# Top-k attention and a gated feed-forward on one core: crossbar transposes queued two slots later, raw weights loaded three chunks ahead, more feed-forward pieces a step

## The chip, the cores and the metric

The kernel runs on one core of a Trainium2 chip. Five engines work side by side, each through its own instructions in order: TensorE (PE) multiplies, VectorE (DVE), ScalarE (ACT) and GpSimd (POOL) work element by element, and SyncE (SP) issues the transfers. They meet through semaphores. The metric is the time of one execution in microseconds (us), as the median of several runs.

## The reference, cut to what matters

```python
# attention: q, k, v are (8, 8, 576, 64) float32
scores = scale * q @ k.T                                  # (8, 8, 576, 576)
kth    = partition(scores, -32)[..., -32]                 # the 32nd largest of each row
scores = where(scores >= kth, scores, -1e9)
attn   = exp(scores - max(scores)); attn /= sum(attn) + 1e-9
x      = (attn @ v) as (4608 tokens, 512)
# feed-forward: w_in (512, 2048) and w_out (2048, 512) are float64
h   = x @ w_in
g   = h * clip(h + 3, 0, 6) / 6
out = g @ w_out                                           # (4608, 512) float32
```

## The kernel before

**Units.** A `Duo` is 128 query rows (a *full* duo) or the 64 leftover rows (a *rest* duo) of four heads, held as two *units* u = 0, 1 of two heads each. There are 80 duos: ten for each of eight batches, of which eight are full and two (the third and the eighth) are rest. The main loop takes *step* m for duo m, and works on its neighbours in the same step: it makes the scores of duo m+1 (`scores`, PE into one large PSUM tile that ACT copies out), finds the 32 largest of each row of duo m (`top`, DVE), and carries duo m-1 and m-2 through softmax and the product with v.

**Slots.** A step has eight slots, `top(0)` to `top(7)`, four for each unit. In a slot DVE takes the eight largest values of each row (`max`, L245) and, in three slots of four, replaces them (`match_replace`, L249); a full duo has two row tiles per unit, a rest duo one. All other work of the step is written between the slots, and this order is the order on every engine, since the kernel schedules by hand.

**From scores to x.** `exp(u)`: POOL makes the threshold and shift (L260 to L262), ACT applies both and sums (L265, L270), POOL adds the epsilon to the sum `den` (L275). `weights(u)`: DVE takes the reciprocal of `den` (L284), POOL scales the rows (L287) and splits their words into two 16-bit halves in tile `e16` (L296), and SP transposes `e16` into `t16` with a crossbar transpose (L299). `join(u)`: ACT puts the halves together in `eT` (L305). `values(m-2)`: PE multiplies by v (L325), and ACT copies the result to `xT` or `xr` (L332).

**Feed-forward.** When 128 or 256 tokens of x are complete they are queued as a block of 16 or 32 *pieces*. A piece is about the same amount of PE work each time: either a half tile of h (L349) or two steps of the output sum (L370). After each full tile of h ACT applies the ReLU (L357) and DVE, more than two pieces later, the gate (L361). `left` counts the pieces queued and not done. Each step runs `count[0]` to `count[3]` pieces at four places; `count` is picked by `level`, from `left` at the step's start. What is left when the 80 duos are done runs at the end.

**Raw weights.** The float64 weights come as 32 chunks of 512 KB. `convert` loads a chunk (`st`, L100, on SP), takes two pieces of it with ACT (L105, L108), clamps with POOL (L106), shifts and merges with two DVE instructions (L114, L115) and adds with POOL (L119). `convert_step` is called in every slot while chunks are left: it finishes an older chunk and starts the next, its load included.

**Order on SP.** SP holds the loads of k and q (`load`, L147, L151), of v (`load_values`, L159, L163), of raw chunks (L100), the crossbar transposes (L299) and the stores of the output (L382), in program order; an instruction that waits holds all that stand behind it. Tiles `st`, `landed`, `kq`, `e16`, `t16` and `eT` share one pool of 14 buffers (`kqpool`).

Of the kernel before, what the change touches and what calls it, by code (L numbers as in the profile page):

```python
# [13 lines left out]
U16 = mybir.dt.uint16  # L14
# [14 lines left out]
def kernel(  # L29
# [9 lines left out]
    nc = tc.nc  # L39
    P = nc.NUM_PARTITIONS  # L40
    B, H, S, D = q.shape
    DM, FF = moe_w_in.shape
    J = S // P
# [8 lines left out]
    def pool(name, bufs, **kw):  # L52
        return ctx.enter_context(tc.tile_pool(name=name, bufs=bufs, **kw))

    consts = pool("consts", 1)
    kqpool = pool("kq", 14)
# [37 lines left out]
    def convert(dst, src):  # L94

        st = kqpool.tile([P, 2 * WC], U32, tag="kq", name="st")
        nc.sync.dma_start(st[:], src)  # L100
        words = st[:].rearrange("p (n two) -> p n two", two=2)
        lo, hi = words[:, :, 0], words[:, :, 1]
        a = gpool.tile([P, WC], F32, tag="g", name="a")
        y = gpool.tile([P, WC], F32, tag="g", name="y")
        nc.scalar.activation(a[:], hi.bitcast(F32), AF.Abs)  # L105
        nc.gpsimd.tensor_scalar(a[:], a[:], HI_MOST, HI_LEAST, ALU.min, ALU.max)  # L106

        nc.scalar.activation(y[:], lo, AF.Copy, bias=2.0, scale=2.0**-51)  # L108
        yield

        au, yu = a[:].bitcast(U32), y[:].bitcast(U32)
        nc.vector.tensor_scalar(au, au, 3, None, ALU.logical_shift_left)  # L114
        nc.vector.scalar_tensor_tensor(  # L115
            out=yu, in0=hi, scalar=0x80000000, in1=yu,
            op0=ALU.bitwise_and, op1=ALU.bitwise_or,
        )
        nc.gpsimd.tensor_tensor(  # L119
            dst.bitcast(I32), a[:].bitcast(I32), y[:].bitcast(I32), ALU.add  # L120
        )

    def weight_chunks():
        win, wout = moe_w_in.bitcast(U32), moe_w_out.bitcast(U32)
        for f in range(0, FF, WC):
            for g in range(NHP):
                rows = slice(g * P, (g + 1) * P)
                yield w_in[:, g, f : f + WC], win[rows, 2 * f : 2 * (f + WC)]
        for c in range(NFC):
            rows = slice(c * P, (c + 1) * P)  # L130
            yield w_out[:, c, :], wout[rows, :]
# [3 lines left out]
    class Pair:  # L135


        def __init__(self, b, hp):
            self.b, self.hp = b, hp
            self.vm, self.vr, self.kr = vms[hp], vrs[hp], krs[b % 2 * NHP + hp]  # L140
# [40 lines left out]
    class Duo:  # L181
# [6 lines left out]
        def __init__(self, pairs, qt):  # L188
            self.pairs, self.qt = pairs, qt
            self.rest = qt == J  # L190
            self.nt = 1 if self.rest else 2
            self.nb = J + 2 if self.rest else 2 * J + 1
            self.t16, self.eT = [None] * 2, [None] * 2

        def scores(self, us=(0, 1)):

# [41 lines left out]
        def top(self, u, r):  # L238

            if r == 0:  # L240
                self.m = mpool.tile([P, 2, TOP_K], F32, tag="m", name="m")
                self.wk = wkpool.tile([P, 2, S], F32, tag="wk", name="wk")
                self.cur = [self.row(u, t) for t in range(self.nt)]
            for t in range(self.nt):
                nc.vector.max(self.m[:, t, 8 * r : 8 * r + 8], self.cur[t])  # L245
            if r < TOP_K // 8 - 1:
                for t in range(self.nt):
                    wk = self.wk[:, t, :]
                    nc.vector.match_replace(  # L249
                        wk, self.m[:, t, 8 * r : 8 * r + 8], self.cur[t], LOWEST  # L250
                    )
                    self.cur[t] = wk
# [24 lines left out]
        def weights(self, u):  # L277

            d = self.den[:, u, 0 : self.nt]
            nc.vector.reciprocal(d, d)  # L284
            for t in range(self.nt):
                row = self.row(u, t)
                nc.gpsimd.tensor_scalar(  # L287
                    row, row, self.den[:, u, t : t + 1], 1.0, ALU.mult, ALU.mult
                )
            n = self.nb * P  # L290
            e16 = kqpool.tile([P, 2 * (2 * J + 1) * P], U16, tag="kq", name="e16")
            halves = e16[:, 0 : 2 * n].rearrange("p (h x) -> p h x", h=2)
            parts = [(0, S + R, 0), (S - P, S, S + R)] if self.rest else [(0, n, 0)]
            for c0, c1, to in parts:
                words = self.sc[:, u, c0:c1].bitcast(U16).rearrange("p (x h) -> p h x", h=2)
                nc.gpsimd.tensor_copy(halves[:, :, to : to + c1 - c0], words)  # L296
            t16 = kqpool.tile([P, 2 * (2 * J + 1), P], U16, tag="kq", name="t16")
            self.t16[u] = t16
            nc.sync.dma_start_transpose(t16[:, 0 : 2 * self.nb, :], e16[:, 0 : 2 * n])  # L299

        def join(self, u):

# [97 lines left out]
    left = 0  # L400
    gates = []

    def piece(count=1):
        nonlocal left
        for _ in range(count):
            while todo:
                try:
                    gates.append(next(todo[0]))
                    left -= 1
                    break  # L410
                except StopIteration:
                    todo.pop(0)
            else:
                gates.append(None)
            if len(gates) > 2:
                gate = gates.pop(0)
                if gate:
                    gate()
# [38 lines left out]
            queue(state["xT"], c0 + P, rows)  # L457

    chunks = list(weight_chunks())
    converting = []  # L460

    def convert_step(depth=1):

        while len(converting) > depth:
            next(converting.pop(0), None)
        if converting and not chunks:
            next(converting.pop(0), None)
        if chunks:
            c = convert(*chunks.pop(0))
            next(c)  # L470
            converting.append(c)

    def pair_at(m, first):

        b, at = divmod(m, per_batch)
        return pairs[b + 1][at - first] if b + 1 < B and 0 <= at - first < NHP else None

    first = pairs[0]
    first[0].load()
    convert_step(2)  # L480
    first[0].transpose()
    duos[0].scores((0,))
    first[1].load()
    convert_step(2)
    first[1].transpose()
    duos[0].scores((1,))
    first[2].load()
    convert_step(2)
    first[3].load()

    for m in range(ND + 2):
        u = duos[m] if m < ND else None
        prev = duos[m - 1] if 0 < m <= ND else None


        level = (left >= 10) + (left >= 20)
        if u and u.rest:
            count = [(1, 0, 1, 0), (1, 0, 1, 1), (1, 1, 1, 1)][level]
        else:
            count = [(2, 1, 2, 1), (2, 2, 2, 1), (2, 2, 2, 2)][level]  # L500
        depth = 2 if m < 2 else 1

        def top(r):
            if u:
                u.top(r // 4, r % 4)
            convert_step(depth)

        if prev:
            prev.exp(1)
        elif m == 0:  # L510
            first[2].transpose()
            first[3].transpose()
        if m + 1 < ND:
            duos[m + 1].scores()
        top(0)
        piece(count[0])
        p = pair_at(m, 4)
        if p:
            p.load()
        if m == 0:  # L520
            first[0].load_values()
            first[1].load_values()
        top(1)
        if prev:
            prev.weights(1)
        if m > 1:
            values(m - 2)
        if u and u.pairs[0].b and 1 <= m % per_batch <= 2:
            for p in duos[m - 1].pairs:
                p.load_values()  # L530
        piece(count[1])
        top(2)
        if prev:
            prev.join(0)
        top(3)
        if u:
            u.exp(0)
        if m == 0:
            first[2].load_values()
            first[3].load_values()  # L540
        piece(count[2])
        top(4)
        p = pair_at(m, 5)
        if p:
            p.transpose()
        top(5)
        if u:
            u.weights(0)
        piece(count[3])
        top(6)  # L550
        if prev:
            prev.join(1)
        top(7)
        if m == 3:
            piece(3)
    while todo:
        piece()
    piece(2)
# [33 lines left out]
```

## Time and profile before

| | us |
|---|---|
| median of three runs (1792.1 to 1793.2) | 1792.3 |
| the profiled execution's own time | 1793.51 |
| its span in the profile | 1791.7 |
| DVE busy (87% of the span) | 1560.9 |
| PE busy (84%) | 1502.2 |
| ACT busy (66%) | 1190.7 |
| POOL busy (41%) | 735.2 |

The profiled execution is 1.8 us longer than its span and 1.2 us above the median. Busy times are means over stages with different limits, so they are read stage by stage.

### The profile page before, as it was taken

The page shows a single profiled execution, that of the slowest core. Times are in us where ns is not written, and L with a number is a line of the kernel's source. Part 1 is how long each engine was busy: PE and PEld are TensorE (multiplying, and loading weights), DVE is VectorE, ACT ScalarE, POOL GpSimd, SP SyncE. Part 2 cuts the span into 40 slices and gives each one's busy share as a digit, 9 for nine tenths or more (in the row PEclk, how much of TensorE's full clock was granted, in tenths as well). Part 3 has the DMA queues.
Part 4 walks back from the last instruction along what each step waited for, and adds up shares of the span by engine and source line. Part 5 has one row for each costly group of instructions (what it writes and reads, how often), then busy time and mean ns, then how long its engine had stood idle before and what let it go on. Part 6 is the DMA issues. An engine that isn't in the chain of part 4 may idle for free.

```text
span 1791.7 us, 24696 instructions
## 1 busy us (share of the span) xinstructions
PE 1502.2 (84%) x8480; PEld 986.7 (55%) x8480; DVE 1560.9 (87%) x3249; ACT 1190.7 (66%) x1639; POOL 735.2 (41%) x1218
## 2 busy tenths in 40 slices
PE   5122767697999999899999899899999899998999
PEld 2012454464665656464756656565666565555575
DVE  3856899999999989999999989999999999999310
ACT  4354687777877777678777777777766877766410
POOL 2565444434444444444344444434443434444100
PEclk9555888799999999999999999999999999999999
DMA  6323343444344433535244442444244533323200
GB/s 184 90 92 121 90 100 63 80 85 92 71 82 88 92 83 54 102 78 109 49 79 90 80 88 49 108 86 91 54 101 82 92 64 73 83 54 70 46 13 12
DMA packets 450302, 144.23 MB, mean 80 GB/s; under 512 B 433280, under 2 KB 441472, under 8 KB 450176
## 3 DMA queue, kind: packets, MB, share of 16 engines
q1 hardware_dynamic: 450176, 142.65, 37.9%
q8 instruction: 67, 1.10, 0.3%
q14 instruction: 59, 0.48, 0.1%
HBM read 45.09 MB, written 9.44 MB: 30 GB/s over the span
## 4 chain that ended last, share of the span: by engine, by line
DVE 64%; PE 14%; ACT 12%; POOL 3%; issue 3%; DMA 3%; SPq 0%; ACTq 0%; POOLq 0%
DVE m L245 32%; DVE wk L249 26%; PE acc L370 7%; DVE g L361 4%; PE h L349 4%; ACT eT L305 3%; ACT sc L270 3%; ACT sc L228 2%; PE big L222 2%; ACT sc L265 2%; PE pv L325 1%; DMA st<-in_moe_w_out_dram 1%; DMA t<-e 1%; DMA st<-in_moe_w_in_dram 1%; POOL a L106 1%
## 5 line engine op out<-in xcount | busy, mean ns | idle before, releaser
L245 DVE MAX8 m<-wk 128x8 f32<-128x576 f32 x864 | 612.5, 744 | 2.0
L370 PE MATMUL acc<-w_out,g 128*128 128x512 f32 x1152 | 523.4, 602 | 6.2 <-DVE g L361 6.2
L349 PE MATMUL h<-xT,w_in 128*128 128x256 f32 (+1 forms) x2304 | 474.8, 364 | 33.6 <-DVE g L361 22.2
L349 PEld LDWEIGHTS h<-xT,w_in 128*128 128x128 f32 x2304 | 402.6, 195 | 90.9 <-issue 19.1
L305 ACT COPY eT<-t 128x2304 uint16<-128x2304 uint16 (+1 forms) x160 | 418.4, 2615 | 39.6 <-DMA t<-e 39.3
L249 DVE MATCH_REPLACE8 wk<-m,wk 128x576 f32<-128x576 f32 x576 | 423.1, 740 | 0.0
L265 ACT ACTIVATE sc<-sc,kth 128x576 f32<-128x576 f32 x288 | 209.1, 768 | 252.3 <-POOL kth L260 252.2
L370 PEld LDWEIGHTS acc<-w_out,g 128*128 128x128 f32 x1152 | 213.2, 192 | 240.0 <-issue 229.3
L296 POOL COPY e<-sc 128x2304 uint16<-128x2304 uint16 (+1 forms) x192 | 321.2, 1683 | 10.1
L287 POOL TENSOR_SCALAR sc<-sc,den 128x576 f32<-128x576 f32 x288 | 214.7, 754 | 269.4 <-DVE den L284 263.9
L325 PE MATMUL pv<-eT,vm 128*64 128x128 f32 (+1 forms) x2560 | 182.2, 285 | 127.2 <-ACT eT L305 87.6
L325 PEld LDWEIGHTS pv<-eT,vm 128*64 128x64 f32 x2560 | 148.1, 148 | 178.0 <-ACT eT L305 93.0
L270 ACT ACTIVATE sc<-sc,shift 128x576 f32<-128x576 f32 x288 | 219.2, 762 | 3.0
L275 POOL TENSOR_SCALAR den<-den 128x2 f32<-128x2 f32 (+1 forms) x160 | 35.5, 222 | 446.8 <-ACT sc L270 446.8
L245 DVE MAX8 m<-sc 128x8 f32<-128x576 f32 x288 | 203.3, 742 | 15.6 <-ACT sc L231 15.6
L249 DVE MATCH_REPLACE8 wk<-m,sc 128x576 f32<-128x576 f32 x288 | 211.5, 740 | 0.0
L222 PE MATMUL big<-kq 64*128 64x512 f32 x512 | 144.0, 685 | 73.9 <-ACT kr L179 34.6
L361 DVE SCALAR_TENSOR_TENSOR g<-g,h 128x512 f32<-128x512 f32 x144 | 96.7, 672 | 106.4 <-ACT g L357 106.2
L357 ACT ACTIVATE g<-h,three 128x512 f32<-128x512 f32 x144 | 97.1, 681 | 88.0 <-PE h L349 87.8
L222 PEld LDWEIGHTS big<-kq 64*128 64x128 f32 x512 | 48.6, 206 | 142.0 <-issue 46.4
L228 ACT COPY sc<-big 128x2048 f32<-128x2048 f32 (+1 forms) x65 | 118.4, 1822 | 11.2 <-PE big L225 10.9
L260 POOL TENSOR_SCALAR kth<-m 128x2 f32<-128x2 f32 (+1 forms) x160 | 36.5, 228 | 116.9 <-DVE m L245 116.4
(45 smaller groups left out, 996.6 us busy)
## 6 DMA issues: line engine op xcount, KB each, us to landing
landed<-in_k_dram SPq DMA_DIRECT2D x64, 128.0 KB, 2.8
landed<-in_q_dram SPq DMA_DIRECT2D x64, 128.0 KB, 2.9
st<-in_moe_w_in_dram SPq DMA_DIRECT2D x16, 512.0 KB, 5.2
vm<-in_v_dram SPq DMA_DIRECT2D x64, 128.0 KB, 2.3
st<-in_moe_w_out_dram SPq DMA_DIRECT2D x16, 512.0 KB, 5.2
out_dram<-o SPq DMA_DIRECT2D x32, 256.0 KB, 2.4
t<-e SPq DMA_TRANSPOSE x160, 4.6
landed<-in_k_dram SPq DMA_DIRECT2D x32, 32.0 KB, 2.6
```

The source lines that it names most:

```text
L222: nc.tensor.matmul(banks[:, 2 * i + hh, :], pr.qT[d, qs], pr.kT[d, :])
L245: nc.vector.max(self.m[:, t, 8 * r : 8 * r + 8], self.cur[t])
L249: nc.vector.match_replace(wk, self.m[:, t, 8 * r : 8 * r + 8], self.cur[t], LOWEST)
L265: nc.scalar.activation(row, row, AF.Prelu, bias=kth[:, t : t + 1], scale=1.0, alpha=STEEP)
L270: nc.scalar.activation(row, row, AF.Exp, bias=shift[:, t : t + 1], scale=scale, accum_out=self.den[:, u, t : t + 1],)
L287: nc.gpsimd.tensor_scalar(row, row, self.den[:, u, t : t + 1], 1.0, ALU.mult, ALU.mult)
L296: nc.gpsimd.tensor_copy(halves[:, :, to : to + c1 - c0], words)
L305: nc.scalar.copy(eT[:, 0 : self.nb, :] .rearrange("p c q -> p (c q)") .bitcast(U16) .rearrange("p (x h) -> p h x", h=2), self.t16[u][:, 0 ...
L325: nc.tensor.matmul(pv[hh * D : (hh + 1) * D, u * w : (u + 1) * w], pr.vm[:, hh, c, :] if c < J else pr.vr[:, hh, :], rhs, start=(c == 0), ...
L349: nc.tensor.matmul(h[:, (f - f0) * nt : (f - f0 + 1) * nt], w_in[:, i, f * P : (f + 1) * P], xT[:, i, 0:nt], start=(i == 0), stop=(i == NH ...
L361: nc.vector.scalar_tensor_tensor(out=g[:], in0=g[:], scalar=6.0, in1=h[:], op0=ALU.min, op1=ALU.mult)
L370: nc.tensor.matmul(acc[:], gs[f // nf][:, c0 : c0 + P], w_out[:, f, :], start=(f == 0), stop=(f == NFC - 1),)
```

## The change

Three things change. The crossbar transpose of a unit leaves `weights` and becomes `flip`: `flip(1)` of the duo before stands after `top(3)` (its `weights(1)` stands after `top(1)`), and `flip(0)` of this duo after `top(7)` (its `weights(0)` stands after `top(5)`). `t16` is allocated there too. The load of a raw chunk is split off from the start of its conversion: `land` issues loads, five of which stand ahead of the main loop, and `convert_step` starts a chunk that was loaded three calls earlier and finishes one that was started two calls earlier. The loads of the first pairs and the first conversions are ordered anew. The table of pieces per step gets a fourth level and other bounds, and three extra pieces at the end of step 3 are dropped.

```diff
@@ convert
         st = kqpool.tile([P, 2 * WC], U32, tag="kq", name="st")
         nc.sync.dma_start(st[:], src)
+        yield
@@ Duo.weights
-            t16 = kqpool.tile([P, 2 * (2 * J + 1), P], U16, tag="kq", name="t16")
-            self.t16[u] = t16
-            nc.sync.dma_start_transpose(t16[:, 0 : 2 * self.nb, :], e16[:, 0 : 2 * n])
+            self.e16[u] = e16
+
+        def flip(self, u):
+            t16 = self.t16[u] = kqpool.tile([P, 2 * (2 * J + 1), P], U16, tag="kq", name="t16")
+            n = 2 * self.nb
+            nc.sync.dma_start_transpose(t16[:, 0:n, :], self.e16[u][:, 0 : n * P])
@@ loading and converting
-    converting = []
-
-    def convert_step(depth=1):
-
-        while len(converting) > depth:
-            next(converting.pop(0), None)
-        if converting and not chunks:
-            next(converting.pop(0), None)
-        if chunks:
+    landing, converting = [], []
+
+    def land(count=1):
+
+        for _ in range(min(count, len(chunks))):
             c = convert(*chunks.pop(0))
             next(c)
+            landing.append(c)
+
+    def convert_step(depth=2):
+
+        if len(converting) >= depth or not landing:
+            for c in converting[:1]:
+                next(c, None)
+            del converting[:1]
+        if landing:
+            c = landing.pop(0)
+            next(c)
             converting.append(c)
+        land()
@@ ahead of the loop
     first[0].load()
-    convert_step(2)
+    first[1].load()
+    land(2)
     first[0].transpose()
     duos[0].scores((0,))
-    first[1].load()
-    convert_step(2)
+    convert_step()
+    first[2].load()
     first[1].transpose()
     duos[0].scores((1,))
-    first[2].load()
-    convert_step(2)
+    convert_step()
     first[3].load()
+    land()
@@ the loop
-        level = (left >= 10) + (left >= 20)
+        level = (left >= 10) + (left >= 18) + (left >= 26)
         if u and u.rest:
-            count = [(1, 0, 1, 0), (1, 0, 1, 1), (1, 1, 1, 1)][level]
+            count = [(1, 0, 1, 0), (1, 1, 1, 1), (1, 1, 1, 1), (2, 1, 2, 1)][level]
         else:
-            count = [(2, 1, 2, 1), (2, 2, 2, 1), (2, 2, 2, 2)][level]
-        depth = 2 if m < 2 else 1
+            count = [(2, 1, 2, 1), (2, 2, 2, 1), (2, 2, 2, 2), (3, 2, 3, 2)][level]
...
         top(3)
+        if prev:
+            prev.flip(1)
         if u:
             u.exp(0)
...
         top(7)
-        if m == 3:
-            piece(3)
+        if u:
+            u.flip(0)
```

## Rows read from the trace of the kernel before

**Rows 1.** The page: busy time of each engine

```profile
PE 1502.2 (84%) x8480; PEld 986.7 (55%) x8480; DVE 1560.9 (87%) x3249; ACT 1190.7 (66%) x1639; POOL 735.2 (41%) x1218
```

**Rows 2.** Windows: length; PE, PEld, DVE, ACT, POOL busy (instructions); PE clock, DMA, GB/s

```profile
59.00:107.50 48.50, 7.34 (x32) 4.11 (x32) 35.16 (x60) 18.97 (x31) 26.34 (x32) 0.50 0.39 112
107.50:154.90 47.40, 9.20 (x52) 5.71 (x52) 25.65 (x42) 21.30 (x30) 26.87 (x31) 0.54 0.38 113
154.90:199.80 44.90, 19.97 (x134) 18.70 (x136) 33.02 (x60) 22.84 (x32) 24.68 (x33) 0.65 0.31 100
...
448.00:1672.00 1224.00, 1134.23 (x6414) 746.53 (x6411) 1180.71 (x2498) 899.15 (x1226) 521.42 (x894) 0.97 0.40 80
1672.00:1792.00 120.00, 115.45 (x590) 75.94 (x588) 9.79 (x15) 18.64 (x24) 3.79 (x4) 0.99 0.06 17
```

**Rows 3.** DVE's waits from 42 to 200 us: total, times, longest

```profile
DVE a L114 <- POOL a L106: 33.1, 9, 9.7
DVE den L284 <- POOL den L275: 13.3, 5, 5.2
```

**Rows 4.** Timeline of SP's queue, 30 to 84 us: start, duration, instruction

```profile
32.61 1.01 SPq L100 DMA_DIRECT2D st<-in_moe_w_in_dram  x2
58.57 2.87 SPq L299 DMA_TRANSPOSE t<-e  x1
61.54 1.95 SPq L100 DMA_DIRECT2D st<-in_moe_w_in_dram  x4
```

**Rows 5.** Timelines of POOL, DVE and ACT, 54 to 75 us

```profile
56.33 2.21 POOL L296 COPY e<-sc 128x2304 uint16<-128x2304 uint16 x1
56.50 2.58 DVE L115 SCALAR_TENSOR_TENSOR y<-st,y 128x512 uint32<-128x512 uint32 x1
...
66.82 0.66 ACT L105 ACTIVATE a<-st 128x512 f32<-128x512 f32 x1 [13.86 <-DMA st<-in_moe_w_in_dram]
...
68.22 1.49 DVE L114 TENSOR_SCALAR a<-a 128x512 uint32<-128x512 uint32 x1 [2.65 <-POOL a L106]
...
74.12 0.17 DVE L284 RECIPROCAL den<-den 128x2 f32<-128x2 f32 x1 [3.40 <-POOL den L275]
```

**Rows 6.** The chain of work that ended last, 50 to 200 us, one piece

```profile
61.54 5.20 DMA st<-in_moe_w_in_dram
```

**Rows 7.** Timelines of ACT and DVE, the start

```profile
9.79 0.66 ACT L105 ACTIVATE a<-st 128x512 f32<-128x512 f32 x1 [7.79 <-DMA st<-in_moe_w_in_dram]
...
39.81 1.49 DVE L114 TENSOR_SCALAR a<-a 128x512 uint32<-128x512 uint32 x1 [10.84 <-POOL a L106]
```

**Rows 8.** The chain of work that ended last, at the end

```profile
1683.96 2.33 PE pv L325 x40
...
1703.66 14.29 PE h L349 x128
1717.95 13.73 PE acc L370 x32
```

**Rows 9.** DVE's waits from 200 to 1672 us

```profile
DVE den L284 <- POOL den L275: 25.7, 30, 3.9
DVE g L361 <- ACT g L357: 13.0, 11, 2.6
```

**Rows 10.** Timelines of ACT and DVE in step 28, the full step after a rest step

```profile
662.45 0.37 ACT L332 COPY xT<-pv 128x256 f32<-128x256 f32 x1 [3.30 <-PE pv L325]
...
666.07 0.60 ACT L380 ACTIVATE o<-acc 128x512 f32<-128x512 f32 x1 [3.25 <-PE acc L370]
...
671.62 0.17 DVE L284 RECIPROCAL den<-den 128x2 f32<-128x2 f32 x1 [3.91 <-POOL den L275]
```

**Rows 11.** Groups by line: busy us, mean ns of one, idle before

```profile
L115 DVE SCALAR_TENSOR_TENSOR y<-st,y 128x512 uint32<-128x512 uint32 x32 | 32.4, 1014 | 0.0
L114 DVE TENSOR_SCALAR a<-a 128x512 uint32<-128x512 uint32 x32 | 26.6, 832 | 44.3 <-POOL a L106 43.9
```

**Rows 12.** Waits of SP's queue over the span

```profile
SPq L382 <- ACT o L380: 133.7, 13, 27.6
```

More of the change, by code (lines that the diff above doesn't have):

```diff
@@ L192, in __init__ @@
             self.nb = J + 2 if self.rest else 2 * J + 1
-            self.t16, self.eT = [None] * 2, [None] * 2
+            self.e16, self.t16, self.eT = [None] * 2, [None] * 2, [None] * 2
         def scores(self, us=(0, 1)):
@@ L505, in top @@
                 u.top(r // 4, r % 4)
-            convert_step(depth)
+            convert_step()
         if prev:
```

## Prediction

> **What bounds the kernel now.** I read the page first: no engine fills the span, DVE with 1560.9 us and PE with 1502.2 us are nearest [rows 1]. A mean of 87% can hide stages with different limits, so next the windows by stage [rows 2]. Three stages show. From 59 to 199.8 us (steps 1 to 3, in which raw weights are converted beside the attention) DVE is busy 35.2 + 25.7 + 33.0 = 93.8 of 140.8 us, and PE hardly at all. From 448 to 1672 us DVE is busy 1180.7 of 1224 us and PE 1134.2: DVE sets the pace, with PE 90 us short of full. From 1672 us to the end DVE has nothing left (9.8 us of work) and PE works off the backlog, 115.5 of 120 us. So time lies in two places: DVE's 47 idle us of the first steps, and the 120 us of PE work behind the last `top`.
>
> **Why DVE idles at the start.** The waits from 42 to 200 us are 46.4 us: 33.1 for POOL's clamp of a raw chunk (L106) and 13.3 for `den` [rows 3]. Followed back, one case reads so. SP issued two raw loads at 32.61 us and then nothing until 58.57, where the transpose of step 0's `weights(0)` started: the next instruction in line was that transpose, and it waited for POOL's split, which began at 56.33 and took 2.21 us. Four raw loads came only behind it, at 61.54 [rows 4, 5]. The first of them was 5.20 us under way, on the chain that ended last [rows 6]; ACT, in order, idled 13.86 us for it, to 66.82; DVE's shift of that chunk waited 2.65 us, and the exponentials that ACT had behind the chunk came late, so that DVE waited 3.40 us more for `den` [rows 5]. This happens once for each unit of steps 0 to 3 until the loads end.
>
> **Part 1, transposes later and loads ahead, at the start: -40 us.** Nothing is removed: 32 loads, 32 conversions and 160 transposes remain. What moves is SP's order: two slots' loads now pass each transpose, and each load is issued three slots ahead of its use. A slot of step 1 without its waits is 35.2 / 8 = 4.4 us [rows 2], so a load has 13 us where it needs 5.2 [rows 6]. The transpose in turn is asked for some two slots (8.8 us) after `weights` was written, and its `join` stands three slots later, so it stays covered at the start. If all waits went, each of steps 1 to 3 would take as long as its busiest engine: 35.2 (DVE), 26.9 (POOL, next to be late in the rest step) and 33.0, together 95.1 for 140.8: -45.7, the lower end. The upper end is 0, if something else holds SP. I take the clamp waits as gone whole (33.1), since the load is what is late in each, and the `den` waits as half gone (6.6 of 13.3), because an exponential still has to pass ACT: -40.
>
> The very start is booked at nothing. ACT no longer waits to 9.79 us for the first raw chunk before it copies the first transposed pair, which can bring 3 us; but conversions now end two calls after they start instead of three, so DVE meets its wait of 10.84 us [rows 7] one slot sooner. Both ends are within 4 us.
>
> **Part 2, the tail: -26 us, and 3 back.** `left` can be followed through the loop on paper, since it depends on the code alone. Take steps 62 to 71: before, 4, 8, 8, 8, 8, 4, 8, 8, 8, 7 pieces, from a backlog of 50 to one of 43; after, 6, 10, 8, 7, 7, 6, 10, 8, 7, 6, from 41 to 30. Behind step 79, the last with a `top`, 52 pieces wait before and 37 after; 16 more come from the last values in both. That is 68 against 53 at the end: 15 fewer. In the tail a block of 128 tokens, 16 pieces, takes 14.29 + 13.73 us [rows 8], 1.75 us a piece. 15 x 1.75 = 26.3 us. (Check: 68 x 1.75 and two products with v of 2.33 are 124 us for a tail of 120.) PE enters the tail later if its last steps are fuller, by less than two pieces: 3 us back.
>
> **Part 3, the fuller steps: +15 us.** The new level is reached in 14 rest steps (6 pieces for 4) and 7 full steps (10 for 8): 42 added pieces, most of them given back as fewer pieces in the steps between. If PE has room, they are free: 0, since DVE sets the pace and PE has 90 us idle [rows 2]. If PE has none, each costs its 1.75 us: 42 x 1.75 = 73.5. What lies between shows in step 28, the full step behind a rest step. There PE was behind DVE; ACT, in order, waited 3.30 us for the product with v and 3.25 for an output sum, the exponentials stood behind both, and DVE waited 3.91 us for `den` [rows 10]. From 200 to 1672 us such waits and the gates' are 38.7 us in all [rows 9]. In the rest steps the two added pieces mostly meet an earlier PE, because the steps ahead of them run 7 and 6 pieces instead of 8 and 7. So I charge the seven full steps of ten pieces, with about 2 us each, half of step 28's stall and a little: 15, nearer to 0 than to 73.5.
>
> Matmul time is what a rule of the Trainium skill distrusts ("Perfetto Trace Analysis", Identifying the Most-Contended Engine): matmul busy time is no good measure of headroom, weight-load time is a better one. By it PE, with weight loads at 55% of the span, would have much room, part 3 would be 0 and the sum 1729. The tail speaks for the price that I use: there PE, with nothing else to wait for, still needs 1.75 us a piece.
>
> **Part 4, flips elsewhere: 0.** From step 4 on no raw loads are left to pass. A flip passes at most a store and, in two steps of ten, eight loads of v. The cover is the three slots up to `join`; without it ACT waits, and DVE for the exponentials behind.
>
> **The sum.** 1793.5 - 40 - 26 + 3 + 15 = 1745.5 for an execution like the profiled one; the median lies 1.2 us lower: **1744 us**.
>
> **Rivals.**
> *PE becomes the bound (slower).* Every added piece lengthens its step by 1.75 us: -40 - 26 + 73.5 gives 1800 us. It decides against the change from 66 / 42 = 1.57 us an added piece upward. For it: step 28's stall. Against it: 90 idle us and steps of 6 and 7 pieces to recover in.
> *The start stays held.* The pool of 14 buffers holds up to 13 tiles by my count with five raw tiles among them; a load may wait for a tile that is only just released, and then three ahead is in truth one ahead: the change would not do what it says. With a quarter of part 1, -10 - 23 + 15 gives 1774 us. For it: POOL's 26.9 busy us of the rest step leave no slack.
> *Stores hold the flips.* SP waited 133.7 us for output sums in 13 cases, 10.3 us each [rows 12]. A store between `weights` and `flip`, about every second, now delays the transpose; if 6 or 7 cost 5 us beyond the cover, that is 34 us: 1778.
> *Conversions get dearer.* The merge L115 takes 1.01 us in the mean [rows 11], but 2.58 when it starts inside POOL's split; the shift L114 0.83, and 1.49 behind a clamp [rows 5]. Packed closer, more of them could meet POOL. All at their longest is 32 x (1.57 + 0.66) = 71 us; half of that gives 1780. Against it: the busy times of part 1 hold the present mix already.
> A rule of the Trainium skill describes this as a lock ("SBUF — State Buffer", Who interferes with whom): DVE, when it needs the port pair shared with GpSimd, is fully blocked until GpSimd's instruction ends. The trace agrees: 56.50 + 2.58 ends 0.54 us behind the end of the split, 56.33 + 2.21.
>
> **How the numbers follow.** Forecast 70%, with a range of its own from 1720 (-45.7, -26.3, 0) to 1768 (about 24 us less gained); start held 11%, stores 7%, dearer conversions 5%, PE bound 5%, anything else 2%. 0.2% of the time is 3.6 us, about what a measurement here can tell from no change. Only the PE bound and half of what is unnamed or worse than priced end above 1796: slower 7%, same 3%, faster 90%. The range, 1720 to 1782, takes in the three middle rivals.
>
> **What would show it.** Right: step 4 begins near 160 instead of 199.8 us; ACT's waits for `st` nearly vanish; the tail behind the last `top` is near 97 us; DVE's waits from step 4 on grow by 10 to 20 us, in steps 23, 28, 43, 48, 63, 68 and 79 and just after. Wrong: waits of L114 that stay, with SP held at L100 by buffers; waits of `den` in every step behind a rest step; ACT waiting for `t16` where it did not.

## The result and the profile after

The changed kernel takes **1734.97 us** (median of 4 runs, 1734.38 to 1737.01); the kernel before took 1792.2 us in the same comparison. The ratio is 0.968, with a 95% interval of 0.967 to 0.970. The forecast was 1744 us, range 1720 to 1782. The profiled execution has a span of 1732.6 us, 59.1 less than before. One run of the experiments, of the kernel with at most eight pieces in a full step, took 4818.32 us and counts in no median below.

Windows of the changed kernel by stage: steps 1, 2 and 3, then the stretch behind the last `max`. Columns as in [rows 2].

```profile
58.20:92.50 34.30, 8.65 (x52) 5.18 (x52) 34.30 (x60) 21.29 (x32) 28.16 (x32) 0.55 0.55 159
92.50:122.90 30.40, 8.09 (x50) 5.16 (x52) 24.32 (x40) 21.16 (x30) 24.41 (x29) 0.56 0.57 172
122.90:155.80 32.90, 18.18 (x154) 15.88 (x150) 32.78 (x61) 18.44 (x28) 26.81 (x32) 0.81 0.26 72
...
1637.60:1732.60 95.00, 91.00 (x542) 65.32 (x538) 8.45 (x14) 19.67 (x26) 4.39 (x7) 1.00 0.10 24
```

Read beside [rows 2]: steps 1 to 3 lasted 140.8 us and now last 97.6, with nearly the same DVE work in them (93.8, now 91.4). DVE idles in step 2 alone. Step 4 begins at 155.8 us instead of 199.8: **44.0 us** less. DVE's last `max` ended at 1668.8 us and now ends at 1637.6, so from step 4 to there it went from 1469.0 to 1481.8 us: **12.8 us** more. What stands behind fell from 122.9 to 95.0 us: **27.9 us** less. The three make the 59.1.

ACT's waits in steps 0 to 3, first of the kernel before (42 to 199.8 us), then of the changed one (42 to 155.8 us): total, times, longest.

```profile
ACT a L105 <- DMA st<-in_moe_w_out_dram: 46.5, 4, 13.0
ACT a L105 <- DMA st<-in_moe_w_in_dram: 26.9, 2, 13.9
```

```profile
ACT sc L266 <- POOL kth L261: 42.2, 7, 8.5
ACT a L106 <- POOL w_in L120: 1.0, 1, 1.0
```

The raw loads have gone from the list. What ACT now waits for, the threshold of the next exponential, POOL makes from DVE's last `max`, so this is DVE's own pace. DVE's waits in the changed kernel from 42 to 155.8 us, to be held against [rows 3]:

```profile
DVE a L115 <- POOL a L107: 4.8, 3, 3.1
DVE den L285 <- POOL den L276: 0.9, 1, 0.9
```

DVE's waits in the changed kernel from step 4 to the last `max`, to be held against [rows 9]:

```profile
DVE g L365 <- ACT g L361: 34.2, 16, 4.5
DVE den L285 <- POOL den L276: 15.0, 15, 2.9
```

Together 49.2 us for 38.7, but their kind has changed: the waits for `den` fell from 25.7 to 15.0 us, and those of the gate rose from 13.0 to 34.2.

The end of the chain that ended last, the counterpart of [rows 8]:

```profile
1618.66 17.36 PE acc L374 x40
1636.03 2.33 PE pv L329 x40
...
1700.58 14.29 PE h L353 x128
1714.87 13.75 PE acc L374 x32
```

A block of 128 tokens still takes 28.04 us; there are fewer of its pieces left.

### The profile page after: what moved, and what is told of

Read it like the earlier page. It is cut to its first block, busy times and chain, and to the rows that moved or that the text cites. A ratio compares the mean times of both kernels' runs of the same rounds, so it can differ in the third digit from the quotient of the medians.

```text
span 1732.6 us, 24693 instructions
## 1 busy us (share of the span) xinstructions
PE 1496.0 (86%) x8480; PEld 984.1 (57%) x8480; DVE 1560.3 (90%) x3249; ACT 1192.7 (69%) x1639; POOL 741.2 (43%) x1218
## 4 chain that ended last, share of the span: by engine, by line
DVE 66%; PE 20%; ACT 8%; POOL 3%; issue 2%; DMA 0%; SPq 0%; ACTq 0%; POOLq 0%
DVE m L246 34%; DVE wk L250 28%; PE h L353 7%; PE acc L374 7%; DVE g L365 3%; PE pv L329 2%; PE big L223 2%; ACT sc L271 2%; ACT eT L309 1%; ACT sc L229 1%; ACT sc L266 1%; POOL w_out L120 1%; ACT g L361 1%; POOL a L107 1%; DVE y L116 1%
## 5 line engine op out<-in xcount | busy, mean ns | idle before, releaser
L353 PE MATMUL h<-xT,w_in 128*128 128x256 f32 (+1 forms) x2304 | 483.7, 368 | 37.2 <-DVE g L365 19.3
L353 PEld LDWEIGHTS h<-xT,w_in 128*128 128x128 f32 x2304 | 407.5, 198 | 97.9 <-DVE g L365 13.9
L288 POOL TENSOR_SCALAR sc<-sc,den 128x576 f32<-128x576 f32 x288 | 218.2, 767 | 299.7 <-DVE den L285 296.4
L329 PE MATMUL pv<-eT,vm 128*64 128x128 f32 (+1 forms) x2560 | 170.0, 279 | 80.7 <-ACT eT L309 56.5
L329 PEld LDWEIGHTS pv<-eT,vm 128*64 128x64 f32 x2560 | 140.2, 145 | 127.2 <-ACT eT L309 62.9
L223 PE MATMUL big<-kq 64*128 64x512 f32 x512 | 140.2, 669 | 62.8 <-ACT sc L216 26.1
```

What stands on the lines that cost most here:

```text
L223: nc.tensor.matmul(banks[:, 2 * i + hh, :], pr.qT[d, qs], pr.kT[d, :])
L288: nc.gpsimd.tensor_scalar(row, row, self.den[:, u, t : t + 1], 1.0, ALU.mult, ALU.mult)
L329: nc.tensor.matmul(pv[hh * D : (hh + 1) * D, u * w : (u + 1) * w], pr.vm[:, hh, c, :] if c < J else pr.vr[:, hh, :], rhs, start=(c == 0), ...
L353: nc.tensor.matmul(h[:, (f - f0) * nt : (f - f0 + 1) * nt], w_in[:, i, f * P : (f + 1) * P], xT[:, i, 0:nt], start=(i == 0), stop=(i == NH ...
```

## Experiments

Each time is a median of four runs, but for the one named above (three), with the kernel before beside it (1794.0 us beside the first four kernels, 1792.3 and 1792.4 beside the others). The rows of the kernel before and of the change are from the comparison above. The runs of one kernel lie within 5 us of one another. "Step 4" is the first `max` of step 4 in the trace.

### The parts one by one

**Flips alone** (kernel before, `flip` as in the change, loads and table as before).

```diff
-            nc.sync.dma_start_transpose(t16[:, 0 : 2 * self.nb, :], e16[:, 0 : 2 * n])
+            self.e16[u] = e16
...
         top(3)
+        if prev:
+            prev.flip(1)
...
         top(7)
+        if u:
+            u.flip(0)
```

> The kernel before with the transposes alone moved two slots later; loads, conversions and the table of pieces stay as before. The whole change started step 4 at 155.8 us where before it was 199.8, 44 us earlier. Theory A (SP's order is what held the loads, the lead only adds cover): the loads of two slots now pass each transpose and only the load of the next slot is still held, so about half of the 44 us returns: step 4 near 175 us, a time near 1767 us. Rival B (the lead of three slots is what helps, the place of the transposes nothing): step 4 stays near 199 us and the time within 5 us of 1792. Rival C (the place of the transposes alone does it all): step 4 near 158 us, time near 1748.

**Loads ahead alone** (flips directly behind `weights`, old table).

```diff
             prev.weights(1)
+            prev.flip(1)
...
             u.weights(0)
+            u.flip(0)
```

> The kernel before with the loads three slots ahead and the new order of the first loads and conversions, but with each transpose directly behind its split as before, and the old table of pieces. Theory A: the lead of three slots covers SP's wait at a transpose, since SP is let go about when the unit's slots end and the held loads are needed a slot or more later; step 4 near 160 us, time 1748 to 1755. Rival B says the same, with nothing left for the flips. Rival C (only the place of the transposes counts): step 4 near 195 us, time near 1788.

**Both, old table.**

```diff
-        level = (left >= 10) + (left >= 18) + (left >= 26)
+        level = (left >= 10) + (left >= 20)
...
+        if m == 3:
+            piece(3)
```

> The change without its table of pieces: flips and loads ahead as in the changed kernel, pieces per step as before. If the three terms add, the start's 44 us are gained and nothing else: 1792.2 - 44 = 1748 us, with step 4 at 156 us and DVE's waits from step 4 on as before (38.7 us). If the flips cost something from step 4 on (a store or a load of v ahead of a transpose), the time is above 1752, with ACT waiting longer for t16.

**The table alone** (kernel before with the new `level` and `count`, without `piece(3)`).

> The kernel before with the new table of pieces alone. If the terms add: 28.0 us less behind the last max, 12.9 us more from step 4 on: 1792.2 - 15 = 1777 us, step 4 at 200 us, DVE's waits for the gate from step 4 on near 34 us instead of 13. If the table works only because the start became shorter, the time stays within 4 us of 1792.

| run | time, us | step 4 at | last `max` ends | behind it |
|---|---|---|---|---|
| before | 1792.2 | 199.8 | 1668.8 | 122.9 |
| flips alone | 1753.06 | 157.7 | 1627.3 | 123.0 |
| loads ahead alone | 1749.31 | 156.9 | 1625.8 | 122.9 |
| both, old table | 1753.03 | 158.0 | 1628.5 | 123.0 |
| table alone | 1774.95 | 199.4 | 1679.0 | 95.0 |
| the change | 1734.97 | 155.8 | 1637.6 | 95.0 |

The start and the table add, within the spread of the runs: -41.0 (both) and -19.1 (table) against -57.2 for the change, each against the kernel before beside it. Within the start nothing adds. Either edit alone gives all of it, and the two together give no more than one. So theory A was right on the loads and wrong on the flips, from which I expected half. Rival B, that the flips do nothing, fell too. Rival C, that their place does it all, came nearest for the flips (step 4 at 158, 1748 us) and fell with the loads, from which it expected almost nothing. SP's queue with flips alone shows why half was too little:

```profile
58.40 2.82 SPq L302 DMA_TRANSPOSE t<-e  x1
61.32 2.31 SPq L100 DMA_DIRECT2D st<-in_moe_w_in_dram  x4
```

The transpose and the loads behind it go within 0.3 us of the times of [rows 4]. What differs is which loads are behind it. Before, those of slots 6 and 7 stood there, which ACT had been asking for since 52.96 us (66.82 less 13.86, [rows 5]); now they have gone ahead, and the first load that is held is the next unit's, which ACT takes at 67.31 us without a wait. With loads ahead alone the held loads are due three slots later. Each edit gives the few us that were missing (44 us over the six loads that ACT waited for are some 7 us each), and a second cover over the first is worth nothing.

The flips may even cost a little. Both against loads alone is 3.7 us slower (1750.57 to 1753.59 against 1747.9 to 1752.33, so the runs overlap), and ACT's longest wait for `t16` from step 4 on is 6.3 us with them, 3.0 without:

```profile
ACT eT L309 <- DMA t<-e: 40.3, 32, 6.3
```

```profile
ACT eT L309 <- DMA t<-e: 36.4, 35, 3.0
```

(The first row is of both, the second of loads ahead alone.)

### What the fuller steps cost, and where

The largest waits of the gate in the changed kernel sit where the forecast put them: 4.5, 2.9, 4.5, 3.4, 1.8 and 2.9 us in steps 23, 28, 43, 48, 63 and 68, 20 us together (step 79, also named, has none before its last `max`). Five rest steps with six pieces have another 11.0 us of such waits, 2.1 to 2.3 us each. This is step 68, timelines of PE, ACT and DVE:

```profile
1401.57 5.34 PE L353 MATMUL h<-xT,w_in 128*128 128x256 f32 x24
...
1403.47 1.87 ACT L229 COPY sc<-big 128x2048 f32<-128x2048 f32 x1
1405.23 0.38 ACT L232 COPY sc<-big 128x256 f32<-128x256 f32 x1
1405.50 0.70 ACT L361 ACTIVATE g<-h,three 128x512 f32<-128x512 f32 x1
1406.23 0.69 DVE L365 SCALAR_TENSOR_TENSOR g<-g,h 128x512 f32<-128x512 f32 x1 [2.92 <-ACT g L361]
```

Three pieces (24 matmuls) stand behind slot 0. The first of them finishes a tile; its gate is written behind the second piece after that one, which is now at the same place. DVE reaches it directly behind its slot, and ACT reaches the ReLU only behind the copy of the scores. By the code the gate stands like this in steps 23, 28, 48 and 68. In steps 43 and 63 (6.3 of the 20 us) the tile was finished one place earlier, with two slots of DVE between. There PE itself was late: in step 43 it had three pieces of an output sum and a product with v in front, and came to that tile only at 919.19 us, when DVE reached the gate. Timelines of PE, ACT and DVE:

```profile
919.19 7.17 PE L353 MATMUL h<-xT,w_in 128*128 128x256 f32 x32
...
922.95 0.69 ACT L361 ACTIVATE g<-h,three 128x512 f32<-128x512 f32 x1 [3.24 <-PE h L353]
...
923.67 0.69 DVE L365 SCALAR_TENSOR_TENSOR g<-g,h 128x512 f32<-128x512 f32 x1 [4.50 <-ACT g L361]
```

Theory G is that this grouping is the cost; rival P, that PE has no room. Four kernels:

**The gate one piece later.**

```diff
-            if len(gates) > 2:
+            if len(gates) > 3:
...
-    piece(2)
+    piece(3)
```

> The changed kernel with one number changed: DVE's gate of a full tile of h is put more than three pieces later instead of more than two. Theory G: what the fuller steps cost DVE is that three pieces now stand at one place, so the gate of a tile finished by the first of them stands at the same place as its own matmuls and DVE has to wait until PE and ACT get there. Then the gate's waits, 34.2 us from step 4 on, fall below 15, and the time falls by 10 to 20 us, to 1715 to 1725. Rival P: PE simply has no room for the added pieces; then the waits move to den or to PE's wait for a free tile, and the time stays within 4 us of 1735.

**Ten pieces as five groups of two.**

```diff
-            count = [(2, 1, 2, 1), (2, 2, 2, 1), (2, 2, 2, 2), (3, 2, 3, 2)][level]
+            count = [(2, 1, 2, 1, 0), (2, 2, 2, 1, 0), (2, 2, 2, 2, 0), (2, 2, 2, 2, 2)][level]
...
+        piece(count[4])
         top(7)
```

> The changed kernel with the ten pieces of the fullest step as 2 + 2 + 2 + 2 + 2 at five places (the fifth before the last slot) instead of 3 + 2 + 3 + 2 at four; the number of pieces in every step is the same. Theory G: no three pieces stand together, the gate's waits in steps 23, 28, 43, 48, 63, 68 (20 us together) nearly vanish, those behind rest steps stay: 1715 to 1722 us. Rival P: the same work in the same step, 1731 to 1739 us.

**Four pieces at most in a rest step**, `(1, 1, 1, 1)` for `(2, 1, 2, 1)`.

> The changed kernel with at most 4 pieces in a rest step instead of 6. By the code 16 full steps instead of 7 then run ten pieces, and 55 pieces instead of 53 are left behind step 79. Theory G: nine more steps with three pieces at one place at about 3.3 us each, less the rest steps' 11 us: about 20 us slower, 1750 to 1760. Rival P (a rest step is what has no room, a full step has some): faster, 1722 to 1733.

**Eight pieces at most in a full step**, `(2, 2, 2, 2)` for `(3, 2, 3, 2)`.

> The changed kernel with at most 8 pieces in a full step instead of 10; rest steps keep 6. By the code 57 pieces instead of 53 are left behind step 79. Theory G: the 20 us of gate waits in the full steps go, 4 x 1.75 = 7 us come back at the end: 1720 to 1726. Rival P: the pieces taken out at 1.75 us each give 24 us and most of them come back in later steps and at the end: 1730 to 1738.

| run | time, us | last `max` ends | behind it | DVE's waits from step 4: gate, `den` |
|---|---|---|---|---|
| the change | 1734.97 | 1637.6 | 95.0 | 34.2, 15.0 |
| gate one piece later | 1739.97 | 1643.2 | 94.9 | 17.2, 36.8 |
| five groups of two | 1714.96 | 1618.7 | 95.0 | 16.3, 14.0 |
| rest steps at 4 | 1751.47 | 1647.2 | 103.8 | 36.8, 20.8 |
| full steps at 8 | 1732.44 | 1626.8 | 104.6 | 19.4, 17.1 |

Five groups decide it. Every step runs as many pieces as in the changed kernel, 95.0 us are left behind the last `max` as before, and 20.0 us are gone. So PE had the room, and P falls. The same place of step 68 in that kernel:

```profile
1384.17 3.62 PE L353 MATMUL h<-xT,w_in 128*128 128x256 f32 x16
1385.24 0.68 DVE L365 SCALAR_TENSOR_TENSOR g<-g,h 128x512 f32<-128x512 f32 x1
1385.84 1.41 DVE L246 MAX8 m<-wk 128x8 f32<-128x576 f32 x2
...
1388.11 0.70 ACT L361 ACTIVATE g<-h,three 128x512 f32<-128x512 f32 x1
1388.85 0.69 DVE L365 SCALAR_TENSOR_TENSOR g<-g,h 128x512 f32<-128x512 f32 x1
```

The ReLU is as late as before (3.94 us behind the start of the first piece, in the changed kernel 3.93); but DVE has a slot's work in front of the gate, and does not wait.

The gate one piece later shows that G as I had stated it was too narrow. The gate's waits halved, to 17.2 us where I had expected less than 15, but those of `den` rose by 21.8, and nothing was gained: the median is 5 us longer, with one of the four runs (1735.31) among those of the change. ACT's waits for PE's h, in the changed kernel and in this one:

```profile
ACT g L361 <- PE h L353: 67.8, 45, 4.1
```

```profile
ACT g L361 <- PE h L353: 83.0, 49, 6.7
```

PE's waits for a gate, ahead of the product with v, in the same two:

```profile
PE pv L329 <- DVE g L365: 24.2, 10, 6.3
```

```profile
PE pv L329 <- DVE g L365: 43.7, 16, 9.6
```

A gate put off keeps its PSUM tile longer (`ps_w` has three), PE waits for it, ACT in order for PE, and the exponentials behind ACT's ReLU come late. That chain is read off the waits; no kernel with a fourth tile was run. So putting off the gate only moves the wait, where regrouping the pieces removes it.

Rest steps at 4 were 16.5 us slower, as G had it and against the rival's "faster", but the sum behind G's number did not hold. I had charged nine further full steps of ten pieces 3.3 us each. Of the 16 such steps the trace has the gate's waits in exactly the ten in which the code puts a gate at the place of its own tile (some 30 us together, 0.55 to 4.60 us each), and none in the other six. With the 11.0 us of the rest steps gone, the gate's waits rose by only 2.6 us and those of `den` by 5.8; 8.8 us more stand behind the last `max`, where the two further pieces are worth 3.5. So three pieces at one place cost DVE a wait at the gate where the gate falls among them, and that the time came into the forecast's range was luck.

Full steps at 8 missed G's range (1720 to 1726) and fell in the rival's (1730 to 1738). The waits lost 12.7 us, not 20, as waits of 1.4 to 2.2 us came up in steps 48, 53, 68 and 73, and 9.6 us came back behind the last `max` where I had 7. Taken alone this run would speak for P; it is the five groups, with the same pieces in every step, that rule P out.

### What was left at the start, and the parts put together

DVE still waits 11.7 us in step 0, once for 9.22 us up to 36.45 us, the counterpart of [rows 7]:

```profile
36.45 1.49 DVE L115 TENSOR_SCALAR a<-a 128x512 uint32<-128x512 uint32 x1 [9.22 <-POOL a L107]
```

**Duo 1's work spread over step 0.**

```diff
-        elif m == 0:
-            first[2].transpose()
-            first[3].transpose()
-        if m + 1 < ND:
+        if m + 1 < ND and m:
             duos[m + 1].scores()
...                                  # first[2].transpose() behind top(1),
...                                  # first[3].transpose() behind exp(0),
...                                  # duos[1].scores() behind weights(0)
```

> The changed kernel with duo 1's work spread over step 0: the third pair's transposes stand behind slot 1, the fourth pair's behind slot 3, duo 1's scores behind slot 5, where all three stood ahead of slot 0. DVE waits 11.7 us in step 0 for the clamp of a raw chunk, whose ACT part stands behind all three. Theory: the wait is ACT's, in order, for PE's transposes and scores; spread over the step each part is covered by the two slots between the start and the end of a conversion, and step 1 starts 6 to 11 us earlier than 58.2; time 1724 to 1729. Rival: the loads are what is late there, or the wait only moves to a later slot; then step 1 starts within 3 us of 58.2 and the time is 1732 to 1738.

It took 1725.47 us, 9.5 less than the change; step 1 begins at 47.7 us instead of 58.2, and DVE's waits for the clamp in step 0 fell from the first of these rows (changed kernel) to the second:

```profile
DVE a L115 <- POOL a L107: 11.7, 2, 9.2
```

```profile
DVE a L115 <- POOL a L107: 2.5, 1, 2.5
```

So the theory held: ACT in order, not a load, was late there.

**Five groups and the spread step 0.**

> Five groups of at most two pieces (1714.96 us) and the spread step 0 together. If they add, 6 to 11 us less: 1704 to 1709. If PE's backlog takes back what DVE gains at the start, less than 4 us less.

1704.17 us: the two add.

**The same with the flips back behind `weights`.**

> As the run with five groups and the spread step 0, but each transpose directly behind its split, as in the kernel before. Loads ahead alone measured 1749.3 us and both 1753.0. Theory: with the loads ahead the later place of the transposes has nothing left to give and costs some us (a store or a load of v ahead of a transpose, a later join): 0 to 4 us faster than the run beside it. Rival: with fuller steps the later place is needed: 3 to 10 us slower.

1702.72 us (1701.9 to 1704.75, beside 1703.13 to 1705.76): with the loads ahead the flips are not needed, in fuller steps neither. Whether they cost anything is not settled; both pairs of runs lean that way and both overlap.

**The same with lower levels** (8, 14 and 20 for 10, 18 and 26, flips kept).

> As the run with five groups and the spread step 0, with the levels at backlogs of 8, 14 and 20 instead of 10, 18 and 26: by the code 21 instead of 7 full steps run ten pieces and 50 instead of 53 are left behind step 79. If PE has room once no three pieces stand together: 3 x 1.75 = 5 us faster than the run beside it. If a full step of ten pieces still costs DVE a wait of some 0.8 us (what is left of it in the five-group run): 14 more steps cost 11 us, 6 us slower.

1701.65 us (1701.54 to 1702.79): 2.5 us faster, half of the 5 expected. The fourteen added steps of ten pieces cost nothing that shows: from step 4 to the last `max` the two kernels take 1462.0 and 1462.2 us. What is missing is behind the last `max`, which fell by 3.5 us (95.8 to 92.3) for three pieces that are worth 5.3. By its median this is the fastest version run, 0.950 of the kernel before (interval 0.948 to 0.952), though its runs overlap with those of the one before it.

## Why the prediction was right, point by point

**Why DVE idles at the start: right.** SP held by a transpose that waits for POOL, raw loads behind it, ACT and DVE behind these: take away either the order or the lack of lead, and steps 1 to 3 lose their waits.

**Part 1, -40: measured -44.0.** Of 46.4 us of waits 5.8 remain, all in step 2, the rest step in which POOL was named as next to be late. The two kinds missed in opposite directions: the clamp waits, booked as gone whole, kept 4.8 us, and the `den` waits, which I kept half, went almost whole (13.3 to 0.9): they were late only through the loads. Another 2.4 us are less DVE work in these steps, which I had not looked for. The forecast treated order and lead as one part and gave them no separate shares; that either is enough, it did not see. The very start, booked at nothing, gave 0.8.

**Part 2, -26 and 3 back: measured -27.9.** PE did not enter the end later, as I had charged. When the last `max` ends PE is in both kernels at the end of the first product with v behind step 79. Three pieces stand ahead of that product now and two before, so 50 pieces are left behind it where there were 66. Sixteen pieces at 1.75 us are 28.0 us; the price was right, and the 3 us back were the error.

**Part 3, +15: measured +12.8.** The size was right and so were six of the seven steps, but the way was not, so the size is in part luck. I took step 28's chain (product with v, exponentials, `den`) as what would grow. `den` shrank by 10.7 us and the gate grew by 21.2, since three pieces at one place put a tile's gate beside its own matmuls (or, in two steps, made PE late for it). Reasoning from the amount of PE work, the forecast did not look at how the pieces are grouped, and so it could not see that 20 us of these waits are free to avoid. The free end of that part, 0, was the nearer one for PE's room: with five groups the stretch from step 4 to the last `max` takes 1463.1 us, 5.9 less than in the kernel before. That end is the one to which the Trainium skill's rule pointed, that matmul busy time is no good measure of headroom ("Perfetto Trace Analysis", Identifying the Most-Contended Engine); those 1463.1 us agree with it.

**Part 4, 0:** right to within 4 us, and if anything a loss.

**The rivals.** PE did not become the bound. The start was not held. Conversions did not get dearer: L115 and L116 take 0.843 and 1.020 us in the mean for 0.832 and 1.014 [rows 11].

```profile
L116 DVE SCALAR_TENSOR_TENSOR y<-st,y 128x512 uint32<-128x512 uint32 x32 | 32.6, 1020 | 0.0
L115 DVE TENSOR_SCALAR a<-a 128x512 uint32<-128x512 uint32 x32 | 27.0, 843 | 16.5 <-POOL a L107 16.5
```

Stores ahead of the flips: this rival was priced from SP's waits over the whole span [rows 12], of which 106.5 of the 133.7 us lie behind the last `max`, where no flip follows. From step 4 to the last `max` SP's waits for output sums are these, first of the kernel before, then of the changed one:

```profile
SPq L382 <- ACT o L380: 27.2, 8, 5.3
```

```profile
SPq L386 <- ACT o L384: 47.9, 21, 6.6
```

They grew, but the longest is 6.6 us, and the transposes did not suffer: ACT's waits for `t16` are 26.0 us there for 35.0 before.

For an execution like the profiled one the forecast was 1745.5 us and 1734.38 was measured, 11.1 less: the three terms missed by 4.0, 4.9 and 2.2 us, all on the same side. Against the median, 1744, it is 9 us.

## What to carry to other kernels

When an in-order queue holds loads behind a waiting transfer, ask by how much the first held load is late. Moving the waiting transfer and issuing the loads earlier buy the same few microseconds, and doing both buys them once. When filler work is handed to an engine between the steps of another, its grouping counts as well as its amount: a consumer placed a fixed number of pieces behind its producer must still have the other engine's own work in front of it. And work that one engine leaves to the end can be priced from the end itself, where little else is running.

## What I had not expected

Putting the gate later gained nothing: the gate's waits fell by 17.0 us and those for `den` rose by 21.8, so a wait was moved and not removed. And a move of two slots in SP's queue, with the first transpose itself starting at almost the same time (58.40 us against 58.57), was worth 41 us.
